# A gated mix of a state-space layer and linear attention: seeds for one residue of the kept states, the last two rows scaled in halves, and a new list of steps

## The chip, the cores and the metric

The kernel runs on one core of a Trainium2 chip. A core has TensorE (PE; its weight loads are shown apart as PEld), VectorE (DVE), ScalarE (ACT), GpSimd (POOL) and SyncE (SP), which here only starts DMA transfers. Matrix products land in PSUM, which has eight banks of 128 partitions by 512 float32 numbers; everything else lies in SBUF. The metric is the device time of one execution in microseconds (us), less is better. Before the change it is 155.13 us, the median of three runs (154.61, 155.14 and 155.13).

## The reference, cut to what matters

Two layers read x (2048 rows, 512 columns) and a gate mixes them row by row:

```python
g = sigmoid((x * gate_w).sum(-1, keepdims=True))
# A: a diagonal complex state space; h has 512 complex states
Lam_bar = exp(dt * Lam);  B_bar = ((Lam_bar - 1) / Lam)[:, None] * Bmat
for t in range(L):
    h = Lam_bar * h + (x @ B_bar.T)[t]
a = 2 * (h_all @ Cmat.T).real + x * Dskip
# B: linear attention, 32 heads of 16; features are softmax(p) and softmax(-p)
q, k, v = split(x @ wqkv);  pq = q @ w_phi;  pk = k @ w_phi
kv = phi_k.T @ v;  z = phi_k.sum(over rows)
b = (phi_q @ kv / (phi_q @ z + 1e-6)) @ wo
out = g * a + (1 - g) * b
```

## The kernel before, in words

**Rows.** The 2048 rows are taken by their residue modulo 8: residue r has 256 rows, two tiles of 128. `x_load` (line 229) transposes a tile from HBM into `xT` through SP's DMA queue.

**The attention part.** Steps `W`, `f` and `w` fold `w_phi` into the key and query weights. Steps `k`, `v`, `q` (line 475) make the projections of one tile: four matrix products of 512 columns in one bank, then a copy to SBUF by ScalarE or VectorE (`evac`, lines 117 to 121). `x`, `n`, `e`, `s` make the features: maxima, minima, exponentials, sums. `a` sums the key features with the values (line 578). For queries, `S1` to `S3` end with four DMA transposes of the features each (`phT`, line 563). `o` is the attention of one tile: two groups of products in a bank each (`pn`, line 736), logarithm and copy on ScalarE, a product on VectorE (line 744) and a transpose, by DMA (line 758) or for tiles 12 to 15 on TensorE (line 753).

**The state-space part.** Eight steps of the recurrence are taken at once. `g` sums, for residue r and a quarter j of the states, what x adds to the state (line 601, eight products of 256 columns; odd residues add earlier sums, lines 606 and 608). The result is kept in SBUF as `uv[j]` (residues 0 to 6), or goes on to the scan `z` (residue 7). `h` (line 660) then makes the state of residue r out of an earlier state and the kept sum: a product with a diagonal matrix `dg` (line 668), to which the kept sum is added in one of two ways. For the residues 1, 2, 4, 5 and 6 (`H_VECTOR`) VectorE adds it when it takes the result out of PSUM (line 672). For residues 0 and 3 TensorE adds it with a product with the identity (line 667), two of 256 columns for each of the four quarters, and ScalarE copies the sum out.

**The output.** `y` sums a tile's states with C (line 717) and Dskip times x (line 722) in one bank `py`; `t` adds the attention's output product to the same bank (line 765), scales the 512 columns by the gate (on ScalarE, line 769, or on VectorE, line 771) and writes the row tile out by DMA (line 773, on SP's queue, or on ScalarE's where the list says `:A`).

**The order.** Each step is a generator. A list written out by hand (`ORDER`) says which step goes on next; `@` names its PSUM bank, `:D` puts a copy or a scaling on VectorE rather than ScalarE, and `F:n` issues n products whose result nobody reads. Each engine runs its instructions in the order of this list, and waits where an input or a bank is not ready. SP's transfers start in the same order.

The step that the change touches most:

```python
add = (r, j) in H_VECTOR
for h in range(2):
    if not add:
        MM(out=ph[:, h, :], lhsT=ident[:], rhs=uv[j][:, r, h, :], start=(h == 0), stop=False, ...)
    MM(out=ph[:, h, :], lhsT=dg[:, ...], rhs=src, start=(add and h == 0), stop=True, ...)
```

Of the kernel before, what the change touches and what calls it, by code (L numbers as in the profile page):

```python
# [23 lines left out]
ORDER = """
NR F:28 NI B W1@0 W0@1 W0 W2@2 W1:D W3@3 W3 f1@4 W2:D f0@5 f2@6 f0 f1:D l10 V@0 F:4 V P f3@1 f3 f2:D F:4 P P k1@2 k1
l13 P2 k0@3 P2 U P2 P2 P2 P2 P4 k2@4 P3 P3 k3@5 P4 P4 k0 v0@0 i0 i2 U i0 i0 i1 i2 k4@7 i0:D i0 k2 i2 i2:D i2 U k3 k5@6
i1 v3@1 n0 x0 l9 i1 V2@2 i3 l12 x0 k4 v2@3 i3 i3 l14 i1 k5 n0 x0 n0 x0 i3 k7@4 n0 x0 U n0 i1 l11 k6@5 n1 x1 x1 n1 x1
n1 l8 R0 R1 x1 i3 k7 M v7@7 x1 n1 n1 k6:D L V2 v1@6 x2 n2 e0 v6@4 v5@5 v4@2 e0 x2 s0 v0 l15 n2 s0 n2 v2 s0 v1 R2 s0 v6
v3 n2 k10@0 k10 s0 k9@3 k9 C4 k13@6 gw D R3 s0 k12@4 e1 v7 s0 e1 s1 C6 k11@1 k11 x2 s1 k14@0 k8@3 k12 k14 k8 v4 k13
a0@71 a0 x2 s1 x2 s1 v5 g00@4 g00 g60@0 n2 x3 s1 g20@3 g60 s1 g10@2 g10 n3 e2 g30@6 g40@5 g10 s1 a1 x3 g20 n3 a1 x3 n3  # L30
x3 g41@4 n3 C3 e2 e2 e2 x3 g30 g40 g30 k15@0 k15 n3 e3 s2 x4 s2 x4 g01@2 g01 e3 e3 s2 g50@3 g11@5 g50 s2 s2 s2 n4 x4
n4 Q3 n4 s2 g50 g21@6 e3 s3 v8@0 g31@2 g11 Q2 g11 n4 g70@3 Q1 s3 C7 g21 g70 v9@5 g70 g70 z0 z0 g31 g31 Q0 w1@6 C0 a2
a2 a2 w0@3 s3 z0 v11@2 v9 g61@5 g41 R4 z0 w1 v8 z0 z0 g61 s3 w2@4 s3 s3 a2 x4 z0 z0 g51@6 g51 x4 w2 C2 s3 w3@0 g51 v11
n4 R5 w3 g71@5 g71 g71 g71 z1 z1 g02@4 g02 g42@6 a3 a3 z0 z0 g42 w0 e4 e4 z1 z1 z1 g62@2 g12@0 q1@5 C1 h50@4 C5 J1 e4
e4 z1 q2@6 q2 g12 g12 g22@3 g22 J0 h50 z1 z1 g62 q3@4 q3 J2 s4 z1 s4 q0@6 z1 s4 q0 q1 xA nA g32@0 J3 g32 g32 h60@3 J0
g52@2 g52 c4 h60 J2 c4 g52 h51@4 c2 s4 s4 g72@6 R7 g72 xA h10@5 nA g72 g72 c2 xA J3 nA h10 v10@0 v10 J1 s4 c5 h51 c5
R6 g23@3 v12@2 c4 c0 c0 g63@5 nA z2 z2 a3 a3 g03@4 xA g03 z2 z2 z2 z2 xA g23 z2 z2 g33@6 c5 v12 z2 z2 g13@0 g13 g63
g43@4 h32@3 g13 nA g43 h52@2 h52 g33 h32 h61@5 h61 h12@0 c0 g53@4 h12 g33 g53 s4 v14@3 c2 eA eA h42@2 h42 g73@6 g53 eA
eA g73 g73 q10@5 sA h11@0 h11 O h00@4 g73 sA v13@2 h00 v13 a4 z3 sA v15@6 z3 v15 h20@0 h01@4 h30@2 v14 h20 sA h30 z3
h31@6 z3 z3 sA a4 h01 h31 c6 c6 sA q13@3 q13 z3 a4 a4 Y Y h22@0 G q10 z3 z3 G q6@2 q6 h22 z3 z3 sA sA Y Y c1 c1 q9@4  # L40
q8@6 q5@7 h62@3 h41@5 c3 h41 c1 c3 c3 h13@0 h62 q11@2 h13 q11 q8 q12@1 c6 q12 h21@5 q5 h21 h02@2 c7 q4@6 q4 h53@3 h53
h23@1 h23 h33@0 h33 sA q9 h40@7 h40 sA q7@5 h43@6 h63@3 c7 h43 q7 c7 y4@0 y4 sA h63 sA h03@1 END h02 o0@4 o0 X1 N1
o1@7 o1 q14@6 X1 N1 h03 o0@5 X1 o1@2 o1 o1 o0 o0 q15@3 o2@4 o2 o2@7 o2 N1 q15 X1 N1 X1 N1 E1 E1 y2@1 y1@2 y1 E1 E1 q14
X2 y0@5 y0 o1 y4 X2 N2 X2 o0 o0 o3@4 o3 o3@7 o3 o1 o3 y2 X2 N2 o2 X2 N2 S1 S1 N2 S1 o3 S1 N2 S1 S1 o3 y5@3 o2 o2 S1 S1
S1 y1 E2 E2 E2 E2 y9@6 G N3 y5 y5 y3@4 y2 X3 X3 N3 t1 G t1 N3 S1 N3 S2 y9 y9 S2 S2 S1 S1 S2 y3 y3 t3 y0 t0 t0 t2 t2
y6@7 X3 t2:A o4@2 o4 o4@5 o4 o4 y6 y6 t3 X3 o4 X3 o4 S2 S2 t3 o5@1 o5 o5@2 o5 o5 y13@5 y13 o5 N3 o6@4 S2 o6 o6@1 o6 o6
y12@2 o5 y7@4 y7 y12 o6 o6 t4 y7 S2 S2 t4:D S2 E3 E3 E3 E3 S2 o7@1 o7 t5 t5 S3 o7@0 o7 S3 o7 t6 S3 o7 S2 o7 y8@1 o8@3
t6 o8 o8@0 o8 o8 S3 S3 y12 t0:A y11@7 o8 o8 o9@3 o9:D o9@0 o9:D S3 y8 y8 o9 o9 S3 S3 o9 o10@3 y11 o10 o10@0 y11 o10
o10 S3 y14@3 S3 y14 t7 t7:D t8 y14 t8 y15@0 o11@4 S3 o11 o11@1 t9 o12@4 o11:D o11 S3 o10 o10 o12 o12@1 o12 o12 t9:D
o11 y15 o13@4 o13:D o13@6 t6:A o13 o13 o11 o12 y10@1 o14@4 y15 o14:D o12@6 t9 o12:D t7:A t1 y10 y10 o13 o15@4 o15  # L50
# [18 lines left out]
def kernel(  # L69
# [46 lines left out]

    def evac(out_ap, in_ap):
        if sel["eng"] == "act":
            nc.scalar.copy(out=out_ap, in_=in_ap)  # L119
        else:  # L120
            nc.vector.tensor_copy(out=out_ap, in_=in_ap)
# [537 lines left out]

    def st_h(r, j):  # L660
        ph = bank([P, 2, NC], F32, "ph")
        add = (r, j) in H_VECTOR
        for h in range(2):
            t = 2 * j + h
            src = hs(r - 1, t, slice(0, NC)) if r in (2, 4, 6) else hs(7, t, slice(-1, NC - 1))
            if not add:
                MM(out=ph[:, h, :], lhsT=ident[:], rhs=uv[j][:, r, h, :], start=(h == 0), stop=False, skip_group_check=True)
            MM(out=ph[:, h, :], lhsT=dg[:, (r + 1) // 2 if r % 2 else 0, t, :], rhs=src, start=(add and h == 0), stop=True, skip_group_check=True)  # L668
# [92 lines left out]
    def st_t(n):  # L761
        ti = order[n]
        py, oT = live["py", n], live["oT", n]
        for g in range(HG):
            MM(out=py[:], lhsT=oT[:, g, :], rhs=Wo[:, g, :], start=False, stop=(g == HG - 1))  # L765
        yield
        ot = pools["op"][1].tile([P, D], BF16, name="ot", bufs=14)
        if sel["eng"] == "act":
            nc.scalar.mul(out=ot[:], in_=py[:], mul=G[:, ti:ti + 1])  # L769
        else:  # L770
            VS(out=ot[:], in0=py[:], scalar1=G[:, ti:ti + 1], scalar2=None, op0=ALU.mult)
# [76 lines left out]
```

## Time and profile before

| what | value |
|---|---|
| median of three runs | 155.13 us (154.61 to 155.14) |
| the profiled execution | 155.28 us |
| its span, first to last instruction | 153.2 us |
| granted TensorE clock, mean | 0.995 |
| PE busy | 146.2 us, 95% of the span |
| DVE busy | 132.4 us, 86% |
| ACT busy | 129.2 us, 84% |

The span leaves 2.1 us of the profiled execution outside. A row of a timeline has the start in us from the span's start, the length in us, the engine (SPq and ACTq are the queues that start DMAs), the line of the kernel, the operation, output<-input, the size and the number of merged instructions; in brackets stands how long the engine was idle before it and what ended that. A row of groups ends with the group's busy time in us and the mean length of one instruction in ns. The table by windows gives for each stretch its length and the busy time and number of instructions of every engine. Instructions on ScalarE and VectorE overlap a little: the next one starts before the last one has ended.

### The profile page before, as it was taken

What the parts mean: (1) busy time and instruction counts of PE and PEld (TensorE: products, weight loads), DVE (VectorE), ACT (ScalarE), POOL (GpSimd) and SP (SyncE); (2) the same over time, 40 slices, a digit from 0 to 9 for tenths busy, and PEclk for the clock granted to TensorE, in tenths of its full rate; (3) what the DMA queues carried; (4) which work ended last, traced back from release to release, by engine and by line L of the source; (5) the groups of instructions that cost most, each with busy time, mean ns of one, the idle gap of its engine ahead of it and who ended that gap; (6) DMA issues with size and microseconds to landing.
All of it is one profiled execution on the core that took longest, in us unless ns stands there. A gap on an engine that the chain in (4) does not pass through costs nothing.

```text
span 153.2 us, 3361 instructions
## 1 busy us (share of the span) xinstructions
PE 146.2 (95%) x1236; PEld 95.0 (62%) x1254; DVE 132.4 (86%) x303; ACT 129.2 (84%) x279; POOL 15.8 (10%) x43
## 2 busy tenths in 40 slices
PE   7899999999999999999999999999999999999990
PEld 7644434788878985869867656555554455555540
DVE  3799999999999999999999999999999958717520
ACT  3489998999998999999998999699498998627562
POOL 8239980000000000000000000000000000000000
PEclk9999999999999999999999999999999999999997
DMA  4875995534445699930000007711278859969842
GB/s 116 164 218 97 223 178 112 103 75 103 103 107 78 129 230 178 166 115 4 0 0 4 0 0 169 74 37 34 42 98 147 176 122 189 162 129 206 247 143 103
DMA packets 50848, 17.55 MB, mean 115 GB/s; under 512 B 44176, under 2 KB 50832, under 8 KB 50832
## 3 DMA queue, kind: packets, MB, share of 16 engines
q1 hardware_dynamic: 48976, 15.75, 53.8%
q10 hardware_dynamic: 1696, 1.57, 3.2%
q8 instruction: 10, 0.16, 0.5%
q0 software_dynamic: 160, 0.01, 0.2%
q14 instruction: 6, 0.05, 0.1%
HBM read 2.64 MB, written 2.10 MB: 31 GB/s over the span
## 4 chain that ended last, share of the span: by engine, by line
PE 78%; SPq 10%; DMA 7%; issue 1%; ACT 1%
PE pgq L601 18%; PE py L717 16%; PE pq L475 9%; PE py L765 8%; SPq L229 8%; PE pv L475 4%; PE ph L668 4%; PE pk L475 4%; DMA xT<-in_A_x_dram 4%; PE kvacc L578 3%; DMA phT<-EEq 3%; PE pn L736 3%; PE pgq L606 2%; PE py L722 2%; PE pgq L608 2%; SPq L284 1%
## 5 line engine op out<-in xcount | busy, mean ns | idle before, releaser
L601 PE MATMUL pgq<-xT,BT 128*128 128x256 bf16 x256 | 31.5, 272 | 0.0
L475 PEld LDWEIGHTS <-xT 128*128 128x128 bf16 x192 | 18.2, 98 | 18.3 <-DMA xT<-in_A_x_dram 0.7
L601 PEld LDWEIGHTS <-BT 128*128 128x128 bf16 x256 | 24.6, 98 | 4.1
L138 ACT ACTIVATE EEk<-EEk 128x1024 bf16<-128x1024 bf16 x20 | 20.4, 1080 | 0.0
L119 ACT CAST uv<-pgq 128x512 bf16<-128x512 f32 x28 | 15.9, 605 | 0.5 <-PE pgq L601 0.4
L475 PE MATMUL pv<-Wv,xT 128*128 128x512 bf16 x59 | 15.5, 379 | 0.3
L475 PE MATMUL pq<-Wq,xT 128*128 128x512 bf16 x60 | 15.4, 379 | 0.2
L765 PE MATMUL py<-Wo,oT 128*128 128x512 bf16 x62 | 15.3, 379 | 0.1
L475 PE MATMUL pk<-Wk,xT 128*128 128x512 bf16 x62 | 14.7, 379 | 0.3 <-DMA xT<-in_A_x_dram 0.2
L138 ACT ACTIVATE EEq<-EEq 128x1024 bf16<-128x1024 bf16 x12 | 11.7, 1042 | 0.3 <-DVE EEq L527 0.3
L769 ACT ACTIVATE ot<-py,G 128x512 bf16<-128x512 f32 x12 | 7.9, 686 | 4.5 <-PE py L765 4.3
L138 ACT ACTIVATE ld<-pn 128x16 f32<-128x16 f32 x32 | 6.1, 191 | 5.7 <-PE pn L736 4.6
L590 ACT ACTIVATE phT<-X,dgB 128x512 bf16<-128x512 bf16 x16 | 10.7, 725 | 0.0
L119 ACT CAST nu<-pn 128x256 bf16<-128x256 f32 x27 | 9.9, 380 | 0.0
L119 ACT CAST vx<-pv 128x512 bf16<-128x512 f32 x16 | 9.1, 604 | 0.4 <-PE pv L475 0.4
L548 DVE TENSOR_TENSOR EEk<-EEk,rck 128x4096 bf16<-128x4096 bf16 (+1 forms) x5 | 9.3, 1858 | 0.0
L744 DVE TENSOR_TENSOR on<-nu,rd 128x512 bf16<-128x512 bf16 x16 | 6.7, 421 | 2.8 <-ACT rd L138 1.6
L765 PEld LDWEIGHTS <-oT 128*128 128x128 bf16 x64 | 5.7, 97 | 5.3 <-DMA oT<-on 0.5
L119 ACT CAST Xq<-pq 128x512 bf16<-128x512 f32 x16 | 8.9, 608 | 0.0
L119 ACT CAST Xq<-pk 128x512 bf16<-128x512 f32 x15 | 8.6, 598 | 0.4 <-PE pk L475 0.4
L736 PEld LDWEIGHTS <-phT 128*128 128x128 bf16 x128 | 6.2, 97 | 3.8 <-DMA phT<-EEq 1.4
L511 DVE TENSOR_TENSOR smk<-smk 128x512 bf16<-128x512 bf16 (+4 forms) x18 | 8.1, 448 | 0.1
(178 smaller groups left out, 321.2 us busy)
## 6 DMA issues: line engine op xcount, KB each, us to landing
X<-HM SPq DMA_DIRECT2D x8, 256.0 KB, 4.5
out_dram<-ot ACTq DMA_DIRECT2D x8, 128.0 KB, 2.5
out_dram<-ot SPq DMA_DIRECT2D x8, 128.0 KB, 2.2
C2r<-in_B_wqkv_dram ACTq DMA_DIRECT2D x2, 256.0 KB, 3.8
Wv<-in_B_wqkv_dram SPq DMA_DIRECT2D x1, 512.0 KB, 4.0
Bn<-in_A_B_re_dram SPq DMA_DIRECT2D x1, 512.0 KB, 5.7
Bn<-in_A_B_im_dram SPq DMA_DIRECT2D x1, 512.0 KB, 6.8
Wo<-in_B_wo_dram SPq DMA_DIRECT2D x1, 512.0 KB, 4.3
```

What stands on the lines that cost most here:

```text
L119: nc.scalar.copy(out=out_ap, in_=in_ap)
L138: ins = nc.scalar.activation(**kw)
L229: nc.sync.dma_start_transpose(out=xT[:, :, ti * P:(ti + 1) * P], in_=x_res[ti // 2, ti % 2])
L475: MM(out=pt[:], lhsT=xT[:, kt, ti * P:(ti + 1) * P], rhs=W[:, kt, :], start=(kt == 0), stop=(kt == KT - 1))
L511: VT(out=dst, in0=cur[:, :, :, 0:n, :], in1=cur[:, :, :, n:2 * n, :], op=op)
L548: VT(out=E5, in0=E5, in1=rc.to_broadcast([P, L, 2 * NB, Dh, 4]), op=ALU.mult)
L590: nc.scalar.mul(out=t_, in_=x_, mul=c_)
L601: MM(out=pg[:, h, :], lhsT=BT[:, kt, 2 * j + h, :], rhs=xT[:, kt, r * NC:(r + 1) * NC], start=(h == 0 and kt == 0), stop=(r % 2 == 0 and k ...
L717: MM(out=py[:], lhsT=hs(r, t, slice(a * P, (a + 1) * P)), rhs=C2B[t], start=(t == 0), stop=False)
L736: MM(out=pn[:, 4 * m:4 * m + 4, :].rearrange("p h e -> p (h e)"), lhsT=ph[:, 4 * hf + m, :], rhs=KVm[:, 4 * hf + m, :], start=(m == 0), st ...
L765: MM(out=py[:], lhsT=oT[:, g, :], rhs=Wo[:, g, :], start=False, stop=(g == HG - 1))
L769: nc.scalar.mul(out=ot[:], in_=py[:], mul=G[:, ti:ti + 1])
```

## The change

Three things change.

1. **Residue 3.** A new set `H_SEED` holds residue 3 for all four quarters. For these, step `h` first copies the kept sum `uv[j][:, r]` into the PSUM bank (with `evac`, which the list puts on ScalarE all four times) and the two products with `dg` then add to what is there. The eight products with the identity are gone. Residue 0 keeps its products with the identity.
2. **The last two rows.** For the output tiles 14 and 15 ScalarE scales columns 0 to 255 and VectorE columns 256 to 511 of the same bank, where one of them scaled all 512.
3. **The list of steps is new from start to end.** Its number of `F` products is the same (36), and so is every other product of TensorE.

```diff
-H_VECTOR = tuple((r, j) for r in (1, 2, 4, 5, 6) for j in range(4))
+H_VECTOR = tuple((r, j) for r in (1,2,4,5,6,) for j in range(4))
+H_SEED = tuple((r, j) for r in (3,) for j in range(4))
@@ st_h
         add = (r, j) in H_VECTOR
+        seed = (r, j) in H_SEED
+        if seed:
+            evac(ph[:], uv[j][:, r])
+            yield
         for h in range(2):
...
-            if not add:
+            if not add and not seed:
                 MM(out=ph[:, h, :], lhsT=ident[:], rhs=uv[j][:, r, h, :], start=(h == 0), stop=False, skip_group_check=True)
@@ st_t
-        if sel["eng"] == "act":
+        if n >= NTI - 2:
+            nc.scalar.mul(out=ot[:, 0:D // 2], in_=py[:, 0:D // 2], mul=G[:, ti:ti + 1])
+            VS(out=ot[:, D // 2:D], in0=py[:, D // 2:D], scalar1=G[:, ti:ti + 1], scalar2=None, op0=ALU.mult)
+        elif sel["eng"] == "act":
             nc.scalar.mul(out=ot[:], in_=py[:], mul=G[:, ti:ti + 1])
@@ ORDER, its beginning
-NR F:28 NI B W1@0 W0@1 W0 W2@2 W1:D W3@3 W3 f1@4 W2:D f0@5 f2@6 f0 f1:D l10 V@0 F:4 V P f3@1 f3 f2:D F:4 P P k1@2 k1
+B NR l10 F:28 W0@0 W1@1 W0:D W1:D W2@2 W2:D W3@3 W3:D f0@4 f0:D f1@5 f1 f2@6 f2 f3@0 V@1 NI V P f3:D P U F:4 P2 k1@2
+V2@3 P2 P2 l8 k2@5 k1 P2 P2 P3 P4 P U P4 V2 P4 U k0@4 k3@1 v2@6 k4@0 P2 P3 v5@2 k2 i2 k0 i0 i3 i2 i3 i2 l9 k3 v4@3 i0
...
@@ ORDER, its end
-o15@6 t4:A t5 o15 o15 t8 o15 t12 t12 t12:A t10 o14@4 o14 o14 t10:D o13@6 t11 o15@2 o15 t10 o13:D t11 t11:A y13 t13 o14
-o14@1 t15 t15 t15 o14:D t14 t13 t13 t14 t14:A
+o14@6 o14 o14 y10@4 t4 t0 o15@5 o15 o15@3 o15 o13 o15 o15 y10 y10 t7:A t10 o13@6 o15@5 o15 o14 o14@3 o14 y15 o13:D t11
+t11:D t13 t10 t10 t11:A t13:D t15 t15 t13 t15 t14 t14 t14
```

What the new list moves, as far as the prediction speaks of it: the four copies of the transposed key weights (`W`, line 276) all go to VectorE, where two went to ScalarE; four of the `F` products go from before the first projection to behind the ninth; the transpose of the fourth block of B (`R3`, line 288) keeps its place among SP's transposes (the 21st) while the product that reads it (`g01`, line 601) comes 0.65 us of TensorE's work sooner; and the third query tile of the first feature group (`o6`) comes 0.65 us sooner behind the start of the list. One of the sixteen scalings of C (line 590) and two absolute values (line 453) go from ScalarE to VectorE.

More of the change, by code (lines that the diff above doesn't have):

```diff
@@ L24 @@
 ORDER = """
-NR F:28 NI B W1@0 W0@1 W0 W2@2 W1:D W3@3 W3 f1@4 W2:D f0@5 f2@6 f0 f1:D l10 V@0 F:4 V P f3@1 f3 f2:D F:4 P P k1@2 k1
[L26 to L49, printed above, removed]
@@ L50 @@
-o11 y15 o13@4 o13:D o13@6 t6:A o13 o13 o11 o12 y10@1 o14@4 y15 o14:D o12@6 t9 o12:D t7:A t1 y10 y10 o13 o15@4 o15
-o15@6 t4:A t5 o15 o15 t8 o15 t12 t12 t12:A t10 o14@4 o14 o14 t10:D o13@6 t11 o15@2 o15 t10 o13:D t11 t11:A y13 t13 o14
-o14@1 t15 t15 t15 o14:D t14 t13 t13 t14 t14:A
-"""
-H_VECTOR = tuple((r, j) for r in (1, 2, 4, 5, 6) for j in range(4))
+B NR l10 F:28 W0@0 W1@1 W0:D W1:D W2@2 W2:D W3@3 W3:D f0@4 f0:D f1@5 f1 f2@6 f2 f3@0 V@1 NI V P f3:D P U F:4 P2 k1@2
+V2@3 P2 P2 l8 k2@5 k1 P2 P2 P3 P4 P U P4 V2 P4 U k0@4 k3@1 v2@6 k4@0 P2 P3 v5@2 k2 i2 k0 i0 i3 i2 i3 i2 l9 k3 v4@3 i0
@@ new lines @@
+v1@5 i2:D F:4 n0 x0 i2 i3 i3:D l13 l12 i0 k4 x0 i1 n0 i3 i1 i1 i0:D i1:D x0 n0 i0 x0 i1 L n0 k5@4 k5 x0 n0 e0 e0 v0@1
+gw k7@0 x1 U x1 l15 n1 k7 x1 n1 k6@7 k6 l14 l11 x1 v5 n1 R0 x1 n1 n1 e1 v6@4 v6 s0 s0 n2 k10@0 v3@7 v3 v2 v7@2 v1 x2
+k9@4 s0 k13@7 n2 x2 s0 x2 R1 s0 M D v0 k8@6 e1 v7 s0 s1 s0 k15@5 n2 C2 R2 s1 n2 R3 k8 k9 k15 k10 k12@1 k14@2 k13 k14
+k12 a0@64 a0 s1 x2 s1 v4 s1 x2 k11@5 C1 k11 Q1 s1 n2 g00@0 g00 Q3 s1 g20@7 Q2 x3 n3 Q0 x3 n3 x3 g10@2 g10 n3 g30@1 a1
+a1 x3 C3 g01@3 n3 x3 C7 e2 g40@5 n3 e2 e2 e2 s2 g10 C0 g20 g40 g41@0 g41 g30 C5 s2 v9@2 g30 s2 g01 n4 s2 R4 e3 e3
@@ new lines @@
+g60@7 g60 s2 n4 g50@5 g50 g50 s2 x4 n4 x4 R5 g11@0 g21@1 n4 s2 e3 e3 g70@3 g70 s3 w0@7 g11 g70 x4 g70 g21 C6 g11 g61@5
+C4 J2 a2 a2 s3 a2 v9 a2 z0 z0 s3 w1@3 x4 g61 s3 g31@1 g31 w0 g31 w1 J3 s3 s3 x4 R6 w3@0 g51@2 w3 z0 v8@5 n4 g51 z0 z0
+J1 g51 J2 w2@7 w2 e4 s3 g71@1 g71 g02@3 g71 g71 z0 z1 z1 q1@0 q0@2 z0 g02 z0 q1 z1 z1 z1 z1 g42@7 e4 q0 e4 g12@1 v8 e4
+g22@3 g22 g12 q3@0 g12 z0 q2@2 z1 z1 q2 v10@5 c5 z0 v10 J0 J0 s4 q3 R7 g32@3 z1 z1 h50@1 g32 s4 g42 g32 c4:D s4 g62@2
+g62 c3 J1 h50 g52@5 g52 g52 h60@0 nA xA g72@7 s4 xA g72 nA c4 c4 h31@3 h51@1 h10@2 a3 h60 xA h51 g72 g72 s4 xA v11@5
@@ new lines @@
+v11 z2 z2 v12@0 J3 c5 s4 c3 g23@7 nA z2 z2 z2 O v12 z2 g23 c3 a3 a3 h32@1 nA a3 c0 z2 z2 g03@5 g13@0 g03 xA h31 h31
+g43@7 z2 c0 g43 g13 g33@5 z2 nA h32 h61@3 h61 v13@7 g13 g33 h32 c0 h10 h12@0 h12 g63@1 eA eA g53@3 s4 g33 g53 g63 v13
+g53 h52@2 h52 h42@0 h42 g73@5 g73 c5 h11@1 h11 h02@7 eA eA sA g73 q11@3 a4 g73 z3 q5@2 z3 h02 h62@0 q5 q11 c2 sA z3 z3
+z3 v14@1 sA z3 v15@5 c1 a4 sA v15 q4@7 z3 q6@2 z3 h30@3 v14 q4 h62 q6 z3 z3 q12@5 sA sA h20@1 h20 h33@7 q12 a4 a4 Y Y
+Y G q10@0 sA sA c2 Y c1 h33 h30 h33 h22@2 h30 q10 h22 c2 sA c1 sA h13@5 h03@1 q14@6 h13 h01@7 h41@3 h01 h43@4 h03 c6
@@ new lines @@
+h53@0 h53 h41 c6 y0@2 h00@7 h00 c6 h21@1 h21 h63@5 c7 h43 q7@0 q8@3 h23@7 h63 h40@1 c7 c7 h40 q7 sA sA q8 q14 q9@4 q9
+h23 END X1 o1@0 o0@5 o0 q13@3 q13 y3@6 o1 o0@1 o0 o0 N1 X1 o1@4 q15@7 o1 N1 G o2@5 X1 y1@3 N1 X1 o1 N1 X1 N1 o2 o2@0
+o2 o2 o2 o1 o1 y2@1 y1 q15 y1 N2 o0 X2 X2 E1 E1 E1 y3 y6@4 E1 o3@5 y5@0 y3 o3 o3@7 y0 o3 o3 N2 o2 o0 N2 G N2 y2 X2 X2
+G S1 t1 S1 S1 y5 o3 o3 t1 t1:A S1 X2 S1 S1 N2 S1 S1 S1 y2 t2 y0 t2 y9@5 y4@7 E2 E2 X3 t0 S1 S1 X3 S1 E2 N3 t0 y6 E2 X3
+t3 N3 t3 t3:A X3 X3 S2 S2 S2 y9 y9 y4 y4 o4@3 o4 o4@1 o4 o4 o4 o4 S2 y13@2 y5 N3 N3 o5@6 o5 o5@3 o5 y6 o5 o5 o5 S2
@@ new lines @@
+t2:A S2 y13 N3 o6@1 o6 o6@6 o6 o6 o6 o6 y12@3 y12 y7@1 y7 t4 S2 E3 S2 S2 S2 S2 t4:D E3 y13 o7@6 E3 E3 S3 o7 t5 S2 o7@7
+S3 S3 o7 o7 t6 t5 t6 y8@6 o7 o7 o8@7 o8 o8@0 o8 S3 o8 o8 S3 S3 y8 o9@4 o9 o9@7 o9:D o8 S3 S3 t5:A S3 y11@0 y11 y12 o9
+o9 o10@4 o10 o9 y8 y14@7 o10@4 o10 y7 t7 y11 t8 t8:D t7 o11@4 o11 o11@1 o11 S3 S3 y14 y14 o10 o12@4 S3 o12:D o12@6 o12
+y15@1 t9 o10 o10 o12 o12 o12@4 o12:D o11 o11 o11 t9 y15 t9 o13@6 o13:D o13@4 o13 o13 t12 t8 t12:D o14@5 t12 t6:A o14
+o14@6 o14 o14 y10@4 t4 t0 o15@5 o15 o15@3 o15 o13 o15 o15 y10 y10 t7:A t10 o13@6 o15@5 o15 o14 o14@3 o14 y15 o13:D t11
```

## The prediction

> **What bounds the kernel now.** I read the page's busy times first, then the chain of work that ended last, then the busy times by window, because an average over 153 us hides where an engine has room.
>
> ```profile
> PE 146.2 (95%) x1236; PEld 95.0 (62%) x1254; DVE 132.4 (86%) x303; ACT 129.2 (84%) x279; POOL 15.8 (10%) x43
> ...
> PE 78%; SPq 10%; DMA 7%; issue 1%; ACT 1%
> ```
>
> ```profile
> 17.00:23.00 6.00, 5.79 (x27) 2.51 (x27) 5.90 (x16) 5.97 (x10) 5.39 (x15) 1.00 1.26 188
> 23.00:40.00 17.00, 16.95 (x161) 12.31 (x161) 16.93 (x34) 16.42 (x31) 0.00 (x0) 1.00 0.48 98
> 40.00:60.00 20.00, 19.84 (x222) 16.20 (x224) 19.84 (x40) 19.19 (x36) 0.00 (x0) 1.00 0.71 141
> 60.00:80.00 20.00, 19.89 (x178) 15.87 (x179) 19.77 (x43) 19.85 (x37) 0.00 (x0) 1.00 0.32 63
> 80.00:96.00 16.00, 15.89 (x138) 10.14 (x139) 15.91 (x37) 15.21 (x33) 0.00 (x0) 1.00 0.20 46
> 96.00:117.00 21.00, 20.84 (x148) 11.26 (x149) 20.82 (x44) 16.89 (x40) 0.00 (x0) 1.00 0.43 59
> 117.00:121.20 4.20, 3.96 (x36) 1.99 (x36) 3.84 (x9) 3.70 (x14) 0.00 (x0) 1.00 1.08 205
> 121.20:135.00 13.80, 13.69 (x109) 7.36 (x112) 9.43 (x16) 10.58 (x31) 0.00 (x0) 1.00 0.80 147
> 135.00:148.40 13.40, 13.29 (x119) 7.63 (x120) 6.80 (x15) 7.57 (x27) 0.00 (x0) 1.00 0.83 197
> ```
>
> The columns are the window, its length, then busy us (and instructions) of PE, PEld, DVE, ACT and POOL, and the granted clock. Length less PE, summed over the nine rows, is 131.40 - 130.14 = 1.26 us: between 17 and 148.4 us TensorE lacks nothing but that, and the clock is 1.00. So TensorE's amount of work sets the time, products taken away count in full, and no wait that goes can give more than 1.26 us. VectorE and ScalarE are nearly full until 96 us and could become the bound.
>
> **The sum, part by part.** It is made against the profiled execution, 155.28 us (span 153.2), which lies 0.15 above the median 155.13.
>
> *The products with the identity.* Eight of 256 columns go. A row by form gives 272 ns for one, but these overlap; their spacing is in the chain, where six `dg` products of that shape take 0.66, 0.11 each.
>
> ```profile
> L667 PE MATMUL ph<-uv,ident 128*128 128x256 bf16 x16 | 3.8, 272 | 0.0
> ```
>
> ```profile
> 90.16 0.66 PE ph L668 x6
> ```
>
> 8 x 0.11 = -0.88 us, all on the bound engine.
>
> *The seeds.* Four copies of 128x512 from bf16 in SBUF to float32 in PSUM are added on ScalarE. Before has no such row. The nearest are a copy the other way, 605 ns, and ScalarE's scaling of the same width, 725 ns; I take 605, since the work differs only in direction. Copies of 0.60 follow each other faster than that: four took 2.04, a spacing of (2.04 - 0.61)/3 = 0.48.
>
> ```profile
> L119 ACT CAST uv<-pgq 128x512 bf16<-128x512 f32 x28 | 15.9, 605 | 0.5 <-PE pgq L601 0.4
> ...
> L590 ACT ACTIVATE phT<-X,dgB 128x512 bf16<-128x512 bf16 x16 | 10.7, 725 | 0.0
> ```
>
> ```profile
> 27.41 2.04 ACT L119 CAST Xq<-pk 128x512 bf16<-128x512 f32 x4
> ```
>
> Four at 0.48 are 1.9 us; one scaling of C and two absolute values leave ScalarE (0.73 for the scaling alone). That adds at most 1.2 between 60 and 96 us, where the windows show 0.15 + 0.79 = 0.94 idle, and 4.11 in the next window. In the new list each seed stands two or more other steps ahead of its products, so TensorE finds it done: cost 0. Without that cover, at 725 ns each with no overlap, ScalarE is 4 x 0.725 - 0.725 - 0.94 = 1.24 us late, and what waits behind a late seed is every later copy out of a bank that TensorE needs next. So 0 to +1.24, and I take 0. Below zero is excluded: TensorE gains nothing from a copy more.
>
> *The start.* All four `W` copies go to VectorE, and four `F` products go behind the ninth projection tile.
>
> ```profile
> 5.13 0.91 DVE L121 COPY Xq<-ptw 128x512 bf16<-128x512 bf16 x2 [0.47 <-PE ptw L274]
> 5.35 1.07 ACT L119 COPY Xq<-ptw 128x512 bf16<-128x512 bf16 x2 [2.18 <-PE ptw L274]
> ...
> 7.10 0.17 DVE L312 CAST vec<-pvt 128x12 f32<-128x12 bf16 x1 [0.34 <-PE pvt L310]
> 7.18 0.68 DVE L121 CAST Wk<-pf 128x512 bf16<-128x512 f32 x1
> 7.45 0.39 PE L812 MATMUL spin<-fillw 128*128 128x128 bf16 x4
> 7.65 0.59 ACT L119 CAST Wk<-pf 128x512 bf16<-128x512 f32 x1
> 7.67 3.62 PE L475 MATMUL pk<-Wk,xT 128*128 128x512 bf16 x15
> ```
>
> ```profile
> 22.89 5.35 PE L475 MATMUL pk<-Wk,xT 128*128 128x512 bf16 x24 [0.16 <-DMA xT<-in_A_x_dram]
> ```
>
> VectorE: 5.13 + 4 x 0.455 = 6.95, first part of `Wk` 7.64, small copy 7.81, last part 8.49, where ScalarE had it at 7.65 + 0.59 = 8.24. The first projection still starts at about 7.67; its fourth product wants the last part at 7.67 + 3 x 0.22 = 8.33 (the 24 products from 22.89 take 0.22 each), so TensorE loses 0.16. Before, the four `F` products at 7.45 fell into a wait; now their 0.22 (the next product follows the four of 7.45 at 7.67) lie on the path. At 22.89 TensorE waited 0.16 for x, and that much of a later arrival is free. 0.16 + 0.22 - 0.16 = +0.22; bounds 0 (more of it disappears in waits before 22.89) and +0.38.
>
> *The transpose of B that keeps its place.* Here are its row on SP in the timeline, its time to landing (from the DMA view of 30.8 to 36.2, which holds only it of `BT`), and the least, median and longest of all eight:
>
> ```profile
> 30.92 2.14 SPq L288 DMA_TRANSPOSE BT<-Bn  x1
> ```
>
> ```profile
> BT<-Bn SPq DMA_TRANSPOSE x1, 3.8
> ```
>
> ```profile
> DMA to landing us min/median/max: 2.5/2.9/5.1
> ```
>
> ```profile
> 35.22 1.03 PE L601 MATMUL pgq<-xT,BT 128*128 128x256 bf16 x8
> ```
>
> It lands at 34.7 and was read from 35.2. Now the reader comes 0.65 sooner, less the 0.22 of the start: 34.8. Cost 0; if the transfer is as slow as the slowest, 5.1, it lands at 36.0 and costs 1.2. I take +0.1.
>
> *The query features.* Four transposes, the third issued behind two that were quick:
>
> ```profile
> 116.71 4.37 DMA phT<-EEq
> ```
>
> ```profile
> 121.13 0.43 PE L736 MATMUL pn<-KVm,phT 128*128 128x68 bf16 x8 [0.18 <-DMA phT<-EEq]
> ```
>
> ```profile
> L563 SPq DMA_TRANSPOSE phT<-EEq x12: 1246/1292/2249, 113.0 to 138.9; - x12
> ```
>
> ```profile
> q8 instruction: 1, 0.02, 0.9%
> ```
>
> One issue took 2.25 us where 1.29 is usual, and TensorE lost 0.24 in the window 117 to 121.2. In the same stretch one packet of instructions was fetched. If that held up the issue (a guess: both fall together once), it will fall on another transfer when the instructions before it change. `o6` comes 0.65 us sooner. Bounds: -0.24 (wait gone) and +0.65 (wait stays, reader sooner). The usual issue is 0.96 shorter, more than the 0.65, so I take -0.2.
>
> *The last two rows.* The end of the chain is the last scaling:
>
> ```profile
> 148.34 0.89 ACT ot L769 x2
> 149.23 0.27 issue
> 149.50 0.69 ACT ot L769
> ```
>
> ```profile
> L119 ACT CAST nu<-pn 128x256 bf16<-128x256 f32 x27 | 9.9, 380 | 0.0
> ...
> L769 ACT ACTIVATE ot<-py,G 128x512 bf16<-128x512 f32 x12 | 7.9, 686 | 4.5 <-PE py L765 4.3
> ```
>
> ```profile
> 138.01 0.20 ACT L138 ACTIVATE ld<-pn 128x16 f32<-128x16 f32 x1
> 138.24 0.42 DVE L121 CAST nu<-pn 128x256 bf16<-128x256 f32 x1 [1.89 <-ACT ld L138]
> 138.91 0.74 DVE L771 TENSOR_SCALAR ot<-py,G 128x512 bf16<-128x512 f32 x1
> ```
>
> Half the width costs ScalarE 0.686 - (0.605 - 0.380) = 0.46, and VectorE 0.74 - (0.68 - 0.42) = 0.48, with its own copies of 512 and 256 columns. If both ran at once the end would come 0.69 - 0.48 = 0.21 sooner. But in the built instructions VectorE's half waits on ScalarE's semaphore for the other half, which is in the same bank. Then they run one after the other: 0.46, a hand-over of 0.03 (ScalarE done at 138.21, VectorE starts at 138.24), 0.48: 0.97 against 0.69, +0.28. Only row 14, the last, stands on the path.
>
> The Trainium skill bears on this ("PSUM — Partial Sum Buffer", section "PSUM bank collisions raise a hardware error"): two engines must not touch one bank in the same 32 partitions at once, two readers included, and the compiler's back end adds a dependency between them. By it the halves give +0.28, without it -0.21; no row of before shows two engines on a bank at once, so the trace neither bears it out nor speaks against it.
>
> *Sum.* -0.88 + 0 + 0.22 + 0.1 - 0.2 + 0.28 = -0.48: 154.8 for a profiled execution like the one shown, and 0.15 less, **154.65**, for the median; I say 154.7.
>
> **The rivals.** Each is a time for the median.
>
> *The waits go too.* The new list may fill the gaps: of the 1.26 us of lost TensorE time half would be 0.6, 154.0 with the sum. If the halves run at once, 0.49 more: 153.6. For it: no gap is long, and each has its own cause. Against it: a new list makes new gaps, and the built instructions show the wait between the halves.
>
> *The third transpose of the features is late (slower or level).* If an instruction fetch or another transfer lies on one of the four that `o6` and its followers wait for, TensorE waits 0.65 more than before: +0.65 in place of -0.2, so 154.65 + 0.85 = 155.5; with a second slow issue, 0.96 more, 156.5. It decides from a landing later than 121.13 - 0.24 - 0.65 + 0.22 (the start) = 120.5 us. For it: the issue of 2.25 that was there before. Against it: it was 1 of 12.
>
> *ScalarE becomes the bound (slower).* If a seed costs 725 ns without overlap, the 1.24 us late reach TensorE between 82 and 96 us: 154.65 + 1.24 = 155.9. It decides once ScalarE's delay passes its 0.94 of idle time plus the lead of the copies. For it: ScalarE is 99% busy from 60 to 80. Against it: VectorE takes a scaling and two absolute values, and the spacing of 0.48 leaves room that the busy time hides. The Trainium skill ("ScalarE: Activation LUTs", section "Step-by-step: what each stage is for") says that ScalarE's way to PSUM is the quicker one; by it this rival is weaker, and no run here shows it.
>
> **How the numbers follow.** The forecast has 0.48, with a range of its own of 154.2 to 155.1; the vanished waits 0.22; the late transpose 0.16; ScalarE 0.14. 0.5% of 155.13 is 0.78 us, about what a measurement of this kernel can tell from no change: faster is below 154.35, slower above 155.91. Of the forecast 0.13 falls below, 0.35 between; the vanished waits are faster; of the late transpose half is slower, of ScalarE's case 0.12, and the rest of the two, 0.10, is level. The range from 153.7 to 155.9 leaves out the best end of the second case and the worse halves of the slow ones.
>
> **What the profile of the changed kernel would show.** 8 `ph<-uv,ident` products; PE busy lower by 0.8 to 0.9. Four ScalarE copies into `ph` of 0.55 to 0.73, and no PE wait on them. First projection at 7.6 to 7.8, its fourth product after 8.4. At the end two halves one behind the other, 0.9 to 1.0 from the last `py` product to the end of the second; at once, 0.5, would refute that step. TensorE idle in 117 to 121 below 0.1, or above 0.5 with a transpose as its cause. ScalarE ahead of TensorE between 82 and 100. The prediction is wrong if TensorE's idle time between 17 and 148 grows by more than 0.6 us at any one place, or if it loses clock.

## The result: half a per cent slower

The changed kernel takes 156.16 us (median of 20 runs, 155.52 to 157.05) and the kernel before, measured beside it, 155.28 us (20 runs, 154.61 to 156.58): a ratio of 1.005, 95% interval 1.0029 to 1.0071. The forecast was 154.7 with a range up to 155.9. The execution profiled here took 155.53 us, one of the quickest of the 20; the one of before took 155.28, just its median. So the two traces show 0.25 us of the 0.88 by which the medians differ. The rest lies in executions of the changed kernel of which there is no trace.

The page of the changed kernel, its busy times and its chain:

```profile
PE 145.6 (95%) x1227; PEld 94.6 (62%) x1246; DVE 133.5 (87%) x307; ACT 129.2 (84%) x281; POOL 16.9 (11%) x43
...
PE 84%; DMA 9%; ACT 2%; SPq 1%; issue 1%; DVE 0%
```

TensorE is busy for 0.6 us less, yet DMA has a larger share of the chain that ended last, 9% in place of 7%, now with the transposes `oT` in it. The windows say where; first one row from 7 to 148.4 us of the kernel before, then rows of the changed one (columns as in the prediction):

```profile
7.00:148.40 141.40, 140.10 (x1178) 90.11 (x1196) 128.69 (x283) 124.52 (x274) 11.63 (x29) 1.00 0.59 114
```

```profile
7.00:148.40 141.40, 138.65 (x1163) 89.14 (x1182) 127.94 (x284) 126.28 (x277) 12.73 (x29) 1.00 0.58 113
...
117.00:121.20 4.20, 3.50 (x45) 2.06 (x44) 3.52 (x9) 2.67 (x13) 0.00 (x0) 1.00 0.94 188
121.20:135.00 13.80, 12.77 (x98) 6.80 (x99) 9.01 (x15) 10.60 (x32) 0.00 (x0) 1.00 0.87 155
```

TensorE's idle time between 7 and 148.4 us grows from 1.30 to 2.75 us. Of these 1.45 us, 0.46 arise in the window 117 to 121.2 (idle 0.70, before 0.24) and 0.92 in 121.2 to 135 (idle 1.03, before 0.11). Behind nearly all of each stands one wait, in the timeline of TensorE:

```profile
117.88 0.43 PE L741 MATMUL pn<-KVm,phT 128*128 128x68 bf16 x8 [0.70 <-DMA phT<-EEq]
134.31 1.04 PE L770 MATMUL py<-Wo,oT 128*128 128x512 bf16 x4 [0.93 <-DMA oT<-on]
```

The first is the attention of tile 4 (`o4`), which needs the first of the query features' transposes; the second is the attention's output product of tile 7 (`t7`), which needs the transpose of its `on`. The DMA views of the moments in which these two were issued (113 to 114 and 129.7 to 130.4 us) give their times to landing:

```profile
phT<-EEq SPq DMA_TRANSPOSE x1, 4.8
...
oT<-on SPq DMA_TRANSPOSE x1, 4.5
```

Usual are 3.2 to 3.3 for the one kind and 2.4 to 2.7 for the other. In both cases the queue `q8`, which the profile calls one of instructions, moved one packet of 16 KB while they were under way: one began at 115.6 us and one at 132.1, and the issue of a transpose at that time took longer as well (2.25 and 1.84 us in place of 1.29). The row of the queue and that of the issue, for the second:

```profile
q8 instruction: 1, 0.02, 5.0%
```

```profile
132.42 1.84 SPq L564 DMA_TRANSPOSE phT<-EEq  x1
```

In the kernel before such packets fell at 114.0 and 132.4 us. They went with late transposes there too (the feature transposes from 113 us on, in the prediction's rows), but at 132.4 nobody had to wait. The product of tile 7 came at 134.53, when the transpose, issued at 130.10, had landed at 134.46; in the trace of before:

```profile
oT<-on SPq DMA_TRANSPOSE x1, 4.4
```

```profile
134.53 1.89 PE L765 MATMUL py<-Wo,oT 128*128 128x512 bf16 x8
```

From here on a fetch is such a packet of `q8`. That it holds instructions of TensorE is inferred: over all twenty traces of this case there lie on average 256 recorded products and weight loads of TensorE between two of them.

### The profile page after: what moved, and what is told of

It reads as the page before. It is cut to its first block, busy times and chain, and to the rows that moved or that the text cites. A ratio compares the mean times of both kernels' runs of the same rounds, so it can differ in the third digit from the quotient of the medians.

```text
span 153.5 us, 3346 instructions
## 1 busy us (share of the span) xinstructions
PE 145.6 (95%) x1227; PEld 94.6 (62%) x1246; DVE 133.5 (87%) x307; ACT 129.2 (84%) x281; POOL 16.9 (11%) x43
## 4 chain that ended last, share of the span: by engine, by line
PE 84%; DMA 9%; ACT 2%; SPq 1%; issue 1%; DVE 0%
PE pgq L602 18%; PE py L722 13%; PE pk L476 9%; PE pv L476 9%; PE pq L476 9%; PE py L770 8%; PE ph L673 4%; DMA phT<-EEq 3%; DMA xT<-in_A_x_dram 3%; DMA oT<-on 3%; PE kvacc L579 3%; PE pn L741 2%; PE pgq L607 2%; PE pgq L609 2%; PE py L727 2%
## 5 line engine op out<-in xcount | busy, mean ns | idle before, releaser
L120 ACT CAST nu<-pn 128x256 bf16<-128x256 f32 x29 | 10.6, 376 | 0.0
L779 DVE TENSOR_SCALAR ot<-py,G 128x512 bf16<-128x512 f32 x5 | 3.8, 751 | 7.2 <-PE py L770 7.1
L777 ACT ACTIVATE ot<-py,G 128x512 bf16<-128x512 f32 x9 | 6.0, 685 | 3.9 <-PE py L770 3.9
```

## Experiments

Theory L: the new list puts readers too early, and only the list's places count. Theory F: a fetch of TensorE's instructions holds up the transposes in flight, and what counts is where it falls. Rivals: the copies ("seeds") hold up ScalarE (S); VectorE sets when the features come, either because it was nearly full already (D) or because the new list gave it more work (V). All ratios are to the kernel before, from runs side by side, with 95% intervals.

### The parts of the change alone

**old_seeds**: the list of before, seeds for residue 3, whole rows.

```diff
+H_SEED = tuple((r, j) for r in (3,) for j in range(4))
-z2 z2 g13@0 ... h32@3 / h30@2 ... h31@6 / h53 h23@1 h23 h33@0 h33
+z2 h32@3 z2 g13@0 ... h32 / h30@2 ... h31@6 ... h30 ... h31 / h33@0 h53 h23@1 h23 h33 h33
```

> The list of before with the seeds alone: four copies of the kept sums of residue 3 into PSUM, each put into the list where its bank is free and a few steps ahead of its products, which stay where they were; the identity products of residue 3 are gone and the last rows are scaled whole. Theory L (the new list makes new waits in the query part, the seeds do what the sum says): 0.88 us less, a ratio to before of 0.994 to 0.995. Theory D (VectorE is nearly full to 113 us and sets when the query features come, so work taken from TensorE ahead of them turns into waiting): 0 to 0.2 us less, with TensorE's idle time between 117 and 121 us up from 0.24 to 0.7 or more. Theory S (the copies hold up ScalarE, and through it TensorE): slower than before, with TensorE idle between 66 and 100 us.

1.0167 (1.0139 to 1.0196), 157.94 us: slower by 2.6 us. In TensorE's timeline, the products wait for the copies:

```profile
85.00 0.39 PE L673 MATMUL ph<-H,dg 128*128 128x256 bf16 x2 [0.76 <-ACT ph L120]
...
96.23 0.38 PE L673 MATMUL ph<-H,dg 128*128 128x256 bf16 x2 [0.90 <-ACT ph L120]
```

That is theory S, 1.66 us of it: a ScalarE that is full to 96 us reaches a seed late when the list puts it only a few steps ahead. (The rest is a later x at 17 to 23 us and late transposes of the attention.) It holds for this list and these places. In the changed kernel each seed stands 13 to 41 steps of the list ahead of its products, here 3 to 7, and no row of TensorE's waits names them; a copy takes 627 ns:

```profile
L120 ACT CAST ph<-uv 128x512 f32<-128x512 bf16 x4 | 2.5, 627 | 0.0
```

**old_halves**: the list of before, the last two rows in halves (the edit of `st_t` alone).

```diff
+        if n >= NTI - 2:
+            nc.scalar.mul(out=ot[:, 0:D // 2], ...)
+            VS(out=ot[:, D // 2:D], ...)
```

> The list of before with only the last two rows scaled in halves. By the sum of the prediction, halves one behind the other: +0.28 us, ratio 1.002. If they ran at once: -0.2 us, ratio 0.999. If the issue of ScalarE's own DMA between two scalings (0.27 us in the chain of before) hides the hand-over: 0.

1.0135 (1.0087 to 1.0184), runs from 156.2 to 159.8 us. The timeline shows a cost that no expectation had:

```profile
149.62 0.47 ACT L769 ACTIVATE ot<-py,G 128x256 bf16<-128x256 f32 x1 [0.95 <-PE py L765]
149.99 0.68 ACT L772 ACTIVATE ot<-py,G 128x512 bf16<-128x512 f32 x1
150.12 0.48 DVE L770 TENSOR_SCALAR ot<-py,G 128x256 bf16<-128x256 f32 x1 [2.06 <-ACT ot L769]
150.53 0.41 DVE L121 COPY oT<-po 128x512 bf16<-128x512 bf16 x1
151.00 1.04 PE L765 MATMUL py<-Wo,oT 128*128 128x512 bf16 x4 [1.42 <-DVE oT L121]
```

In the list of before, a copy of `oT` on VectorE stands behind the scaling of row 15. With halves VectorE waits there for row 15's products and for ScalarE's half, the copy waits behind it, and TensorE waits 1.42 us for the copy. The new list has the copies ahead. That is about half of the loss; the other wait of this size is for a transpose of the attention:

```profile
PE py L765 <- DMA oT<-on: 1.4, 1, 1.4
```

It lands after 5.7 us in place of 4.4. The edit stands far behind it, and the fetch came at 132.4 as in before; but the packet of 8 KB on the other instruction queue, `q14`, took 1.9 us in place of 0.5. So landings differ from execution to execution even where the list ahead of them is the same, and the place of the fetch alone does not tell the wait.

**new_whole**: the changed kernel, the last two rows whole on ScalarE (the three lines above taken out).

> The changed kernel with the last two rows scaled whole by ScalarE. By the sum 0.28 us faster than the changed kernel: ratio to before 1.003 in place of 1.005. If the halves cost nothing: 1.005. If they gain 0.2: 1.006.

1.0036 (1.0011 to 1.0061); against 1.005 this is within the uncertainty, but the ends of the two traces give the size, one execution each. Changed kernel, then whole rows:

```profile
146.24 3.40 PE L770 MATMUL py<-Wo,oT 128*128 128x512 bf16 x15
149.67 0.47 ACT L774 ACTIVATE ot<-py,G 128x256 bf16<-128x256 f32 x1 [0.39 <-PE py L770]
150.18 0.48 DVE L775 TENSOR_SCALAR ot<-py,G 128x256 bf16<-128x256 f32 x1 [0.38 <-ACT ot L774]
```

```profile
147.09 3.40 PE L770 MATMUL py<-Wo,oT 128*128 128x512 bf16 x15
150.53 0.69 ACT L774 ACTIVATE ot<-py,G 128x512 bf16<-128x512 f32 x1 [0.18 <-PE py L770]
```

From TensorE's end it is 150.66 - 149.64 = 1.02 us with halves and 151.22 - 150.49 = 0.73 whole: halves cost 0.29. The halves do run one behind the other, 0.04 us apart, as the Trainium skill has it for one bank ("PSUM — Partial Sum Buffer", section "PSUM bank collisions raise a hardware error"). This trace also had a wait that the changed kernel's did not, for the transpose of B, with a fetch at 32.5 us:

```profile
35.01 1.70 PE L602 MATMUL pgq<-xT,BT 128*128 128x256 bf16 x14 [0.53 <-DMA BT<-Bn]
```

**new_ident**: the changed kernel with identity products where the seed's copy stood.

```diff
         if seed:
-            evac(ph[:], uv[j][:, r])
+            for h in range(2):
+                MM(out=ph[:, h, :], lhsT=ident[:], rhs=uv[j][:, r, h, :], start=(h == 0), stop=False, ...)
             yield
```

> The changed kernel with the products with the identity back: they stand in the list where the seed's copy stood, and the copies are gone. Theory L: 0.88 us more than the changed kernel, ratio to before 1.011. Theory D: the products fall into waiting that is there anyway, 0 to 0.3 us more, 1.005 to 1.007. Theory S: faster than the changed kernel, below 1.004.

1.0098 (1.0067 to 1.0130): slower than the changed kernel, against theory S, and nearest to theory L's 1.011. The 16 instructions that come back also move the fetches (to 114.5 and 133.5 us), so the run was repeated with 16 fewer at the start.

**new_ident_f16**:

```diff
-F:28
+15 products of 128 columns and five of 512
```

> The changed kernel with the products with the identity in place of the seeds (16 instructions of TensorE more), and at the start 15 products of 128 columns and five of 512 in place of 28 (16 instructions fewer): from the last seed on the fetched packets fall at the same instructions as in the changed kernel. This prices the eight products without moving the fetches. The sum of the prediction: +0.88 us against the changed kernel, ratio to before 1.0107. If the waits at the transposes swallow what TensorE gains ahead of them: 0 to 0.3 us, 1.005 to 1.007.

1.0105 (1.0070 to 1.0139), close to the sum (1.0107): 0.0055 above the changed kernel, 0.85 us, with some 0.004 (0.6 us) of uncertainty. So the eight products cost time and the waits at the transposes do not swallow it, for they stay and come later; but 0.85 fits 0.88 without pinning it down, and a part may come from the wide products at the start (below). TensorE's waits in it, an execution of 158.01 us, the slowest of the nine:

```profile
PE py L771 <- DMA oT<-on: 2.3, 1, 2.3
...
PE pn L742 <- DMA phT<-EEq: 0.6, 1, 0.6
```

### The waits: VectorE, the list, or the fetch

**new_dve**: the changed kernel with work put back from VectorE to ScalarE.

```diff
-i0:D i1:D ... c4:D
+i0 i1 ... c4
```

> The changed kernel with one scaling of C and two absolute values put back from VectorE to ScalarE, about 0.9 us of VectorE's time ahead of the query features. Theory V (VectorE's added work sets when the features come, and so the wait at 117 us): the first feature transpose starts up to 0.9 us earlier than at 113.0 against TensorE's products, the wait of 0.70 us falls below 0.2 and the time by 0.3 to 0.7. Theory F: the wait is the fetch upon the transposes; it stays within 0.2 us of 0.70, and the time within 0.2 us.

1.0081 (1.0049 to 1.0113), slower, and the wait for the features is nearly the same (0.62 us; 0.70 in the changed kernel):

```profile
PE py L770 <- DMA oT<-on: 1.4, 1, 1.4
...
PE pn L741 <- DMA phT<-EEq: 0.6, 1, 0.6
PE pk L476 <- ACT Xq L120: 0.5, 1, 0.5
```

The first feature transpose was issued at 113.77 us, 0.74 later than in the changed kernel, and TensorE came to its reader about 0.7 later too. Against TensorE's products it came no earlier, as theory V had asked, so nothing here bears that theory out. The last row is a new wait, for a copy by ScalarE at 20.7 us, which has no room for the work put back at that place; and the wait of `t7` grew from 0.9 to 1.4.

**new_t7**: two steps of `y14` (1.1 us of products) ahead of `t7`.

```diff
-o10@4 o10 y7 t7 y11 t8 ... S3 S3 y14 y14 o10
+o10@4 o10 y7 y14 y14 t7 y11 t8 ... S3 S3 o10
```

> The changed kernel with the last two steps of y14 (1.1 us of TensorE's work that needs nothing late) put ahead of the attention's product of tile 7, before which TensorE waited 0.93 us. Either theory: this wait falls to about 0. Theory L: the time falls by 0.9, to a ratio of 0.999, as the list's places were the cause. Theory F: the stalled queue also holds up what comes behind, so part of the wait turns up at the next reader of a transpose: 0.3 to 0.9 less.

1.0038 (1.0018 to 1.0058). The wait of `t7` is gone, but the time falls by 0.2 us only, which is within the uncertainty and a miss for both theories (0.9, and 0.3 to 0.9). Others have come, in TensorE's waits:

```profile
PE pn L741 <- DMA phT<-EEq: 0.7, 1, 0.7
PE pn L741 <- ACT nu L120: 0.4, 1, 0.4
PE py L770 <- issue: 0.2, 1, 0.2
```

So taking away a wait by the place of one reader does not give its time back, as theory L asked. The second and third row are not in the changed kernel's trace and probably come from the new places of `y14` and its neighbours, so this run does not tell the theories apart.

**new_f14, new_f34, old_f14, old_f34**: nothing but the dummy products at the start (`F`, whose result nobody reads).

```diff
-F:28   (28 of 128 columns)
+f14: 16 of 128 columns and five of 512    f34: eleven of 512
```

> The changed kernel; of the 28 products of 128 columns at its very start (nobody reads them) 16 stay, and five of 512 columns take the place of the other twelve. TensorE is kept busy as long, but its program is 14 instructions shorter ahead of everything else. Theory F (fetch): the packets of 16 KB by which TensorE's instructions are fetched come after fixed numbers of its instructions; in the changed kernel they fell at 115.6 and 132.1 us, upon the transposes of the query features and of the attention, and made them land 1.5 to 2 us late; TensorE waited 0.70 and 0.93 us for these. 14 instructions are about 1 us of TensorE's program there, so the packets come at 116.6 and 133.1, behind the first feature transposes and behind the transpose that the wait of 0.93 was for: both waits fall below 0.3 and the time by about 1.2 us, to a ratio to before of 0.995 to 0.999. Theory L (the list alone puts the readers too early for VectorE and the queue): waits and time as in the changed kernel, 1.005.

> As the run before, with eleven products of 512 columns in place of all 28: 34 instructions fewer, so by theory F the packets come some 2.4 us later than in the changed kernel, at 118 and 134.5 us. Theory F: both waits gone too, 1.0 to 1.4 us less than the changed kernel, unless the second packet makes another transpose late (those for tiles behind the seventh are read from 138 us on). Theory L: 1.005 as the changed kernel.

> The kernel before with the same 14 instructions fewer at the start. Its packets fell at 114.0 and 132.4 us; by theory F they come at about 115 and 133.4: the second and third feature transposes stay late, TensorE's idle time between 117 and 121 us stays between 0.1 and 0.6, the attention's transposes land earlier but had no wait of TensorE's behind them: a ratio of 0.998 to 1.002. Theory L: 1.000, with the transposes' landings unchanged.

> The kernel before with eleven products of 512 columns in place of the 28 at the start, 34 instructions fewer. Theory F: the packets come some 2.5 us later than before's 114.0 and 132.4, at 116.5 and 135 us: the first feature transposes and the attention's three at 130 to 134 us land earlier, the third or fourth feature transpose later; the wait of 0.24 us at 121 goes or stays, so 0 to 0.5 us less than before, ratio 0.997 to 1.000, and not the 1.006 of 14 instructions fewer. If products of 512 columns at the start cost time by themselves (a rival of theory F for the run with 14 fewer): 1.006 or more here too, with eleven of them.

new_f14 1.0016 (0.9990 to 1.0042), new_f34 1.0024 (0.9997 to 1.0051), old_f14 1.0062 (1.0041 to 1.0084), old_f34 1.0073 (1.0044 to 1.0103). All four miss theory F's figures: new_f14 and new_f34 got faster by less than it asked, the two old ones slower where it asked for no change or a gain. In new_f14 the first fetch falls at 118.0 and the wait for `t7` is gone. In old_f14 a wait of 0.9 us for an attention transpose appeared. But the wide products cost time at the start, when eleven of them took

```profile
1.11 4.79 PE L823 MATMUL spin<-fillw 128*128 128x512 bf16 x11 [1.11 <-DVE fillw L158]
```

0.43 us each (the 28 narrow ones 0.11), so that both f34 kernels began their first projection 0.8 to 1.0 us late. That may hide a gain of as much in new_f34, and old_f34 came out as its rival said. The test was made again without them.

**new_F21, old_F21, new_F14**: fewer of the same products.

```diff
-F:28
+F:21   (14 instructions fewer)      F:14   (28 fewer)
```

> The changed kernel with 21 in place of 28 products at its start, all of 128 columns: 14 instructions of TensorE fewer, and TensorE idle for 0.8 us before its first real work. Theory F: the fetch of 115.6 comes at 117 to 118 us and that of 132.1 at 133 to 135; the waits of 0.70 and 0.93 fall below 0.4 in sum, ratio to before 0.999 to 1.002 as in the run with 14 instructions fewer. Rival (the wide products of that run did it, or chance): waits and time of the changed kernel, 1.005.

> The kernel before with 21 in place of 28 such products. Theory F: the fetch of 132.4 falls upon the attention's second transpose of that stretch, as in the run with 14 instructions fewer, and TensorE waits 0.5 to 1.0 us for it at 135 us: ratio 1.004 to 1.008. Rival: 1.000, without that wait.

> The changed kernel with 14 such products, 28 instructions fewer. Theory F: the fetches come at about 119 to 120 and 135 us; the first three feature transposes and those for tile 7 land in time, the fourth feature transpose and the next of the attention are late: 0.998 to 1.003. Rival: 1.005, or more if the idle TensorE begins its work at a lower clock.

new_F21 1.0020 (0.9995 to 1.0045), just within what theory F asked. Its fetches fall at 118.9 and 135.3. The transpose for `t7` lands after 2.5 us (DMA view of 129.9 to 130.6), and TensorE's idle time from 121.2 to 135 is 0.08 us in place of 1.03; the third feature transpose is now the late one:

```profile
oT<-on SPq DMA_TRANSPOSE x1, 2.5
...
121.20:135.00 13.80, 13.72 (x113) 7.59 (x114) 8.95 (x15) 10.78 (x33) 0.00 (x0) 1.00 0.83 168
...
PE pn L741 <- DMA phT<-EEq: 0.9, 2, 0.7
```

old_F21 1.0073 (1.0047 to 1.0098), with the wait that theory F asked for. TensorE's fetch falls at 132.3, hardly earlier than in before, with the work 0.3 us ahead. Behind it comes a packet of 8 KB on `q14`, at 133.1, which takes 1.6 us; before's, at 132.6, took 0.5. The second of the attention's transposes is caught for 5.0 us (issued at 131.2; the first, issued at 129.9, lands in time), and TensorE waits for it:

```profile
oT<-on SPq DMA_TRANSPOSE x1, 5.0
...
q14 instruction: 1, 0.01, 33.4%
```

```profile
136.21 1.04 PE L765 MATMUL py<-Wo,oT 128*128 128x512 bf16 x4 [0.78 <-DMA oT<-on]
```

new_F14 1.0054 (1.0032 to 1.0076) is a miss: the wait for `t7` is gone as expected, but the fetch at 119.0 makes the third feature transpose land after 5.1 us, and TensorE waits 1.3 us in all for the features.

The same edit, seven dummy products left out, makes the one kernel about 0.3% faster (at the edge of the uncertainty) and the other 0.7% slower, and turns their order round: 1.000 against 1.005 with 28, 1.0073 against 1.0020 with 21. That is clear of the uncertainty and rules out theory L as the whole account. The start of the first projection does not explain it: in the traces it moved the other way, 0.5 us later in the kernel that got faster and 0.3 earlier in the one that got slower.

In the new list the landings go with the fetch from run to run. In fourteen traces of it, the transpose for `t7` landed after 3.5 to 5.5 us in the eight where a fetch began while it was in flight, and after 2.5 to 3.4 in the other six; the first feature transpose after 3.5 to 4.8 in six with a fetch, and after 3.2 in the eight without. In the old list, which of the two packets made the difference is open. Over all twenty traces, of the 40 packets of 16 KB that began between 105 and 141 us, 39 had a transpose in flight that landed after more than 3.9 us. By itself that says less than it seems, since a late transpose is in flight for longer; but of the 428 transposes issued in that stretch, 92 of the 111 with such a packet took more than 3.9, and 15 of the 317 without. Nothing showed how a fetch holds up a transpose, or that it is the fetch itself and not something that comes with it; that stays open.

### Is the new list better with its fetches elsewhere?

**new_f14_whole**: new_f14 and new_whole together.

> The changed kernel with 14 instructions fewer at the start and the last two rows scaled whole: the two edits that each made it faster. By their sum, 1.0016 less 0.0014 = 1.000. If it beats before, it is below 0.998.

0.9985 (0.9952 to 1.0019): level with before.

**new_best, new_best22, new_best19**: whole rows, the copies `W1` and `W3` back on ScalarE, the four `F` products behind the ninth projection left out, and 25, 22 or 19 products at the start.

```diff
-F:28 ... W1:D ... W3:D ... i2:D F:4 n0
+F:25 ... W1 ... W3 ... i2:D n0        (F:22, F:19)
```

> The changed kernel with the last two rows scaled whole, two of the four copies of the transposed key weights on ScalarE as in before, the four products behind the ninth projection left out and 25 in place of 28 at the start (14 instructions fewer in all from there on). By the terms: 1.0016 (14 fewer) - 0.0018 (whole) - 0.0014 (0.22 us for the four products) - 0 to 0.001 (the start) = 0.997 to 0.999.

> new_best with 22 in place of 25 products at its start, 6 instructions fewer. Theory F: the fetch of 132.7 comes at about 133.5 to 135, behind the transpose for tile 7; its wait of 1.1 us falls below 0.3, that for the third feature transpose grows from 0.3 to at most 0.7: 0.3 to 0.8 us less than new_best, ratio to before 0.992 to 0.996. Rival (the place of the fetch does not decide): 0.997 as new_best.

> new_best with 19 products, 12 instructions fewer. Theory F: as with 22, the fetches later by another 0.4 us or less; 0.992 to 0.996. Rival: 0.997.

0.9973 (0.9945 to 1.0002), as expected, then 1.0001 (0.9977 to 1.0025) and 1.0028 (1.0005 to 1.0051). With 22 the fetch came at 133.4 and the wait for the attention's transposes stayed at 1.2 us in sum, only for others of them; with 19 that wait is gone, but the first projection starts at 8.2 us in place of 7.0 in new_best's trace, and 0.6 us of waiting for the features is left. The last two expectations failed: moving the fetch did not bring the gain that theory F asked for. No version is shown to beat the kernel before.

## Why the prediction was wrong

By its own steps:

- **The products with the identity, -0.88.** Right as far as the runs can tell: 0.85 in new_ident_f16 against the changed kernel, with 0.6 of uncertainty; and TensorE's busy time is 1.0 higher in new_ident's trace and 0.6 higher in before's than in the changed kernel's, with the same eight products more.
- **The seeds, 0.** Right for the new list. A copy takes 0.627 us, between the bounds 0.605 and 0.725, and no less than a copy of that size out of PSUM in the same trace (0.617). The rival of a late ScalarE was real where the seeds had less lead (old_seeds).
- **The start, +0.22.** Its 0.16 did not come: the last part of `Wk` was ready at 7.90 and not at 8.49, and the first four products ran through from 7.52 to 8.56. The 0.22 for the four `F` products is not settled. The first projection starts at 7.3 to 7.8 us in the eight traces whose first products are unchanged, in the changed kernel at 7.52 and in before at 7.67, and that spread is larger than the term.
- **The transpose of B, +0.1.** Right in kind: no wait in the changed kernel's trace, 0.53 in that of new_whole, within the bound of 1.2.
- **The query features, -0.2.** This step failed: the wait did not go, it grew from 0.24 to 0.70, to +0.46. The rival of a late transpose had its mechanism (+0.65), and the runs with other numbers of dummy products bear out the guess under it as far as that transposes are late where a fetch falls. Two things were wrong. The long issue of 2.25 us was not that of the third transpose, which TensorE waited for, but that of the second (114.37 to 116.62 in before); the third, issued at 116.71 in the usual 1.28, still landed only after 4.37. And the usual issue was taken because the fetch "will fall on another transfer": it fell on the same four again, the first landed after 4.8 us, and now TensorE waited for that one.
- **The last two rows, +0.28.** Right against whole rows in the same list (0.29). Against before it did not count, since before's chain lost 0.27 us between its last two scalings, where the new list has none: from TensorE's end to the last scaling's end it is 1.02 us in both traces.
- **What was not in the sum.** The transpose for `t7`: +0.92, put at nothing without a reason. It is a growth of more than 0.6 us at one place, which the prediction itself had named as a sign of being wrong. I had asked which reader comes sooner only for `g01` and `o6`. Before had no wait there, but only 0.07 us to spare (134.46 to 134.53), because that transpose was already late there, with a fetch beside it. A list that brings TensorE there about a microsecond sooner finds the transfer where it was.

The two waits, 0.66 and 0.92 against the forecast, are more than the gain of 0.48. Between the two profiled executions the balance is: products -0.88 and the four `F` products +0.22, both as in the sum, idle time between 7 and 148.4 us +1.45, the first projection 0.15 earlier: +0.64 at TensorE's last product, which ends 0.47 later (149.64 against 149.17). 0.17 us are left unexplained. From there to the end of the span it takes 0.14 us less, so the span is 0.32 longer and the time 0.25. The median lies 0.88 above. That the slower executions wait longer in the same places is likely but not shown, as no other execution of the changed kernel has a trace; in two near relatives of it `t7` waits 1.5 us (new_whole, an execution of 156.09 us) and 1.4 (new_dve, 156.75).

## What to carry to other kernels

Where one engine is full and transfers feed it late, work taken off that engine arrives as a wait unless the transfers come sooner too: for every transfer that is read within a microsecond of its landing, ask what time it lands and not whether before waited for it. An edit that changes the number of an engine's instructions moves its instruction fetches. Here leaving out seven dummy products moved the time of one kernel by 0.7%, and that of the other perhaps by 0.3% the other way; a difference of this size between two kernels is only the edit's own if it holds with the fetches shifted, by some dummy instructions more or fewer. And an engine that gets half of another's work waits in its own order: look at what is queued behind the half.

## What the runs showed of the hardware that I had not expected

A packet of 16 KB on the instruction queue `q8` goes with a hold-up of the DMA transposes in flight. Between 105 and 141 us, in the twenty traces, the features' transposes land after 4.5 us in the median with such a packet and 3.3 without, the attention's after 4.3 and 2.5; the longest took 6.9 (old_halves). Issues of 1.8 to 2.8 us in place of 1.2 to 1.3 go with it too: each of the 37 transposes behind 100 us whose issue took 1.8 us or more had a packet of `q8` or `q14` beside it. Those of `q8` come about every 9 to 22 us in these traces and, behind 100 us, mostly later when some of TensorE's instructions are left out ahead (115.6 in the changed kernel, 118.9 in new_F21; but the second of the old list 132.4 in before and 132.3 in old_F21). The Trainium skill ("Runtime: NRT & Kernel Launch", section "Instruction fetch mechanics") says that instructions come in blocks of 16 KiB by a DMA queue of the engine's own, at a cost that is mostly hidden. The size agrees, and no wait of TensorE in these traces is put down to its own instructions; the waits of up to 2.3 us that go with the packets are for transposes.
